# Last V group as the stationary side, last K loaded one transfer earlier, output projections as quarters: a decode-attention kernel whose end alone is not bound by DMA

## The chip, the cores and the metric

The kernel runs on one core of one Trainium2 chip. The metric is the device time of one execution in microseconds (us). Each ratio below is against the kernel before on the same chip in the same rounds; kernels of different batches are compared through it. Single executions of one kernel differ by up to 3 us (0.2%). The device time of an execution is 1.8 us longer than the span from its first to its last profiled instruction (1318.72 against 1316.9 us for the profiled one before); traces and table rows marked "span" give the shorter number.

## The reference

```python
# x [8,1,576]; k_cache, v_cache [8,32,4096,128]; wq [576,4096]; wo [4096,576]; all bf16
q = (x @ wq).reshape(8, 1, 32, 128).transpose(0, 2, 1, 3)
p = softmax(einsum("bhqd,bhkd->bhqk", q, k_cache) * 128 ** -0.5)
a = einsum("bhqk,bhkd->bhqd", p, v_cache)...reshape(8, 1, 4096) @ wo
b = gelu(layernorm(x) @ w1 + b1) @ w2 + b2
g = sigmoid((x * gate_w).sum(-1))
out = g * a + (1 - g) * b
```

K and V together are 537 MB and are read once. Everything else is small.

## The kernel before

One group is one batch element and four heads: 64 groups (`g` = 0 to 63), each with 4 MiB of K and 4 MiB of V, each in two alternating buffers. Partition 32h+p holds 128 keys of head h. The vector engine multiplies K by q, the matrix engine (PE) adds up the products in four chunks (`mult`), the vector engine reduces them (`reduce`), softmax follows. In a matrix product, one operand is loaded into PE as weights (the stationary side) and the other is streamed through (the moving side); a column tile is one of the four groups of 32 output partitions to which a small product can be sent (four of them start within 0.01 us of each other in the trace before, at 1305.91). The results stand in an accumulation memory (`psb` in the traces) until they are copied out (evicted). The values product has the probabilities as the stationary side (16 columns) and V as the moving side (512 columns); its result must be evicted and gathered by further matmuls.

```python
def pv(g, part, parts):                      # values product
    s = g % 2
    for land, t0, t1 in v_land[g]:
        ...
            p_pv[g] = matmul(o_ps[s][32*j:32*j+16, :], lhsT=P[:, s, 4 key slots, :],
                             rhs=VB[s][:, 4 key slots, :])        # 32 of them, on four column tiles
    v_done[g] = p_pv[g]                      # releases the V buffer

def evict(g): ...                            # scalar engine: o_ps -> O_sb
def gather(g): ...                           # 4 fp32 matmuls (8 passes): O_sb -> oz_ps, O transposed
def total(g): ...                            # ones matmul: sums of the probabilities over partitions
def norm(g): ...                             # reciprocal, multiply -> OT_sb

for g in range(NG):                          # NG = 64
    if g >= 1:
        if g + 1 < NG:
            load_k(g + 1)                    # waits for k_done(g-1)
            load_v(g)                        # waits for v_done(g-2)
        else:
            load_v_pieces(g)                 # last V in pieces of 64, 32, 16, 16 key slots
    def between(c):                          # behind chunk c of the scores on PE
        if c == 0 and g >= 2: gather(g - 2)
        if c == 1 and g >= 1: rowsum(g - 1); norm(g - 2); total(g - 1)
        if c == 2: ...                       # pieces of the projections
        if c == 3 and g >= 1: pv(g - 1, 0, 1); evict(g - 1)
    scores(g, between)
    if g + 1 < NG: q_of(g + 1)
    softmax(g)
gather(62); norm(62); rowsum(63); total(63); pv(63, 0, 1); evict(63); gather(63); norm(63)
a_proj(7)              # last four heads: 8 matmuls, 8-column weights, 288 moving columns
...                    # two output operations on 8 x 288, one store
```

(`gather(62)` and the like stand for the source's `gather(NG - 2)`; the matmul calls are shortened.)

## Time and profile before

| | before |
|---|---|
| time, median of the first three runs | 1317.06 us (1316.98 to 1318.01) |
| span of the profiled execution | 1316.9 us |
| DMA | 557.76 MB, mean 424 GB/s |
| last K landed / exponentials of group 63 end | 1284.1 / 1304.6 us |
| last piece of V landed | 1303.2 us |

From the page of the kernel before: busy shares, two rows of the 40 slices (busy tenths, and GB/s), and the chain of waits.

```profile
PE 897.5 (68%) x5204; PEld 428.9 (33%) x5204; DVE 871.6 (66%) x1058; ACT 204.5 (16%) x394; POOL 2.3 (0%) x11
...
DMA  9999999999999999999999999999999999999994
GB/s 398 428 429 430 431 430 429 429 430 433 432 429 431 433 428 430 420 427 430 430 430 430 432 430 432 433 431 430 431 430 431 430 430 429 431 432 431 432 433 190
...
DMA 64%; DVE 18%; PE 17%; ACT 1%; issue 0%; SPq 0%
```

DMA is full in 39 of 40 slices. Only the last slice is open. The transfer view of the last 77 us of the kernel before (from 1240 us, 1.93 us a digit) shows it more finely:

```profile
DMA  9999799998989999899998989989955510000000
GB/s 443 443 417 477 340 477 392 443 494 357 494 374 460 447 392 494 374 460 426 392 511 349 477 357 443 455 375 404 375 247 230 234 81 0 0 9 0 0 0 5
```

Seven of the 16 DMA engines have run ahead and are done by about 1297 us. The other nine finish near 1303 us. The last 13.5 us carry no K or V at all. The timeline of the kernel before, from the issue of the last V (start, duration, engine, line, operation, and in brackets the idle time before it and what ended it):

```profile
1281.32 2.29 SPq L183 DMA_DIRECT2D VB<-in_A_v_cache_dram  x4
...
1284.12 4.49 DVE L342 TENSOR_TENSOR p<-KB,q_bc 128x4096 bf16<-128x4096 bf16 x2 [2.70 <-DMA KB<-in_A_k_cache_dram]
...
1299.70 1.90 PE L402 MATMUL psb<-VB,P 128*16 128x512 bf16 x32
...
1302.28 2.33 ACT L384 ACTIVATE P<-s_sb,mD 32x128 bf16<-32x128 f32 x4
...
1304.64 0.69 DVE L390 TENSOR_REDUCE rs<-P 128x4 f32<-128x512 bf16 x1 [0.85 <-ACT P L384]
...
1305.91 3.59 PE L402 MATMUL psb<-VB,P 128*16 128x512 bf16 x32
...
1309.55 0.60 ACT L415 ACTIVATE O_sb<-psb 128x512 f32<-128x512 f32 x1 [4.94 <-PE psb L402]
...
1310.20 1.87 PE L420 MATMUL psb<-sel,O_sb 128*128 128x4 f32 x8 [0.70 <-ACT O_sb L415]
...
1312.56 2.08 PE L486 MATMUL psb<-RB,OT_sb 128*8 128x288 bf16 x8 [0.49 <-DVE OT_sb L427]
1313.71 0.51 DVE L551 SCALAR_TENSOR_TENSOR out_sb<-psb,stat,up 8x288 bf16<-8x288 f32 x1 [1.21 <-PE psb L486]
1314.67 0.50 DVE L551 SCALAR_TENSOR_TENSOR out_sb<-psb,stat,up 8x288 bf16<-8x288 f32 x1 [0.45 <-PE psb L486]
1315.21 0.31 SPq L183 DMA_DIRECT2D out_dram<-out_sb  x1
```

The reader should see one chain: the last K lands, scores and softmax take 20 us, and all of V has landed before its probabilities are ready. So the end of this kernel waits for the K side. The V side has slack: the last completion write of V comes at 1303.2, and the four matmuls that alone need the last piece start only at 1308.9.

### The profile page before, as it was taken

What the parts mean: (1) busy time and instruction counts of PE and PEld (TensorE: products, weight loads), DVE (VectorE), ACT (ScalarE), POOL (GpSimd) and SP (SyncE); (2) the same over time, 40 slices, a digit from 0 to 9 for tenths busy, and PEclk for the clock granted to TensorE, in tenths of its full rate; (3) what the DMA queues carried; (4) which work ended last, traced back from release to release, by engine and by line L of the source; (5) the groups of instructions that cost most, each with busy time, mean ns of one, the idle gap of its engine ahead of it and who ended that gap; (6) DMA issues with size and microseconds to landing.
All of it is one profiled execution on the core that took longest, in us unless ns stands there. A gap on an engine that the chain in (4) does not pass through costs nothing.

```text
span 1316.9 us, 12176 instructions
## 1 busy us (share of the span) xinstructions
PE 897.5 (68%) x5204; PEld 428.9 (33%) x5204; DVE 871.6 (66%) x1058; ACT 204.5 (16%) x394; POOL 2.3 (0%) x11
## 2 busy tenths in 40 slices
PE   3457776787748678647776676686666676586667
PEld 1123443343323334323333233232233233233323
DVE  3576676676747676746676776776676677667664
ACT  1201111111110110101111101101101101111111
POOL 0000000000000000000000000000000000000000
PEclk8777878868778798767877877878887887877786
DMA  9999999999999999999999999999999999999994
GB/s 398 428 429 430 431 430 429 429 430 433 432 429 431 433 428 430 420 427 430 430 430 430 432 430 432 433 431 430 431 430 431 430 430 429 431 432 431 432 433 190
DMA packets 24726, 557.76 MB, mean 424 GB/s; under 512 B 2368, under 2 KB 6496, under 8 KB 7008
## 3 DMA queue, kind: packets, MB, share of 16 engines
q1 hardware_dynamic: 24496, 556.95, 98.7%
q8 instruction: 41, 0.67, 0.2%
q14 instruction: 13, 0.11, 0.0%
q10 hardware_dynamic: 176, 0.03, 0.0%
HBM read 556.96 MB, written 0.01 MB: 423 GB/s over the span
## 4 chain that ended last, share of the span: by engine, by line
DMA 64%; DVE 18%; PE 17%; ACT 1%; issue 0%; SPq 0%
DMA KB<-in_A_k_cache_dram 64%; DVE p L342 14%; PE psb L352 13%; PE psb L420 3%; DVE s_sb L357 3%; PE psb L402 1%; ACT P L384 0%; DVE rz L426 0%; DVE OT_sb L427 0%; ACT O_sb L415 0%; PE psb L486 0%; SPq L183 0%; ACT L455 0%; DVE rs L390 0%; PE psb L409 0%
## 5 line engine op out<-in xcount | busy, mean ns | idle before, releaser
L352 PE MATMUL psb<-p,ident 128*128 128x512 bf16 x2048 | 651.1, 476 | 398.5 <-DVE p L342 398.5
L342 DVE TENSOR_TENSOR p<-KB,q_bc 128x4096 bf16<-128x4096 bf16 x256 | 579.6, 2285 | 177.8 <-DMA KB<-in_A_k_cache_dram 174.8
L352 PEld LDWEIGHTS psb<-p,ident 128*128 128x128 bf16 x2048 | 226.4, 121 | 713.0 <-DVE p L342 430.6
L357 DVE TENSOR_REDUCE s_sb<-psb 128x32 f32<-128x512 f32 x256 | 175.7, 687 | 106.1 <-PE psb L352 105.5
L415 ACT ACTIVATE O_sb<-psb 128x512 f32<-128x512 f32 x64 | 38.2, 597 | 1065.4 <-PE psb L402 1065.4
L384 ACT ACTIVATE P<-s_sb,mD 32x128 bf16<-32x128 f32 x256 | 147.0, 574 | 5.8 <-DVE mD L381 1.9
L402 PE MATMUL psb<-VB,P 128*16 128x512 bf16 x2048 | 123.5, 383 | 0.0
L420 PEld LDWEIGHTS psb<-sel,O_sb 128*128 128x128 f32 x512 | 106.1, 287 | 24.5 <-issue 16.7
L426 DVE RECIPROCAL rz<-psb 128x4 f32<-128x4 f32 x64 | 11.7, 183 | 137.1 <-PE psb L420 137.1
L420 PE MATMUL psb<-sel,O_sb 128*128 128x4 f32 x512 | 92.1, 303 | 1.4 <-ACT O_sb L415 1.4
L402 PEld LDWEIGHTS psb<-VB,P 128*16 128x16 bf16 x2048 | 45.9, 90 | 71.8 <-issue 28.4
L390 DVE TENSOR_REDUCE rs<-P 128x4 f32<-128x512 bf16 x64 | 43.5, 680 | 0.9 <-ACT P L384 0.9
L409 PEld LDWEIGHTS psb<-rs,ones 128*128 128x128 f32 x128 | 31.3, 245 | 18.0 <-issue 9.5
L409 PE MATMUL psb<-rs,ones 128*128 128x4 f32 x128 | 21.1, 235 | 2.0 <-DVE rs L390 2.0
L440 PEld LDWEIGHTS psb<-yT_sb,RB 128*128 128x128 bf16 (+1 forms) x216 | 19.4, 165 | 3.3
L336 ACT ACTIVATE q_bc<-psb 128x128 bf16<-128x128 f32 x64 | 17.4, 272 | 18.3 <-PE psb L334 18.3
L440 PE MATMUL psb<-yT_sb,RB 128*128 128x8 bf16 (+1 forms) x216 | 19.8, 227 | 0.0
L375 DVE TENSOR_REDUCE mA<-s_sb 128x1 f32<-128x128 f32 x64 | 18.3, 287 | 2.2
L334 PEld LDWEIGHTS psb<-Q,Sel 128*128 128x128 bf16 x64 | 6.1, 95 | 27.3 <-issue 26.7
L381 DVE STREAM_TRANSPOSE mD<-mC 128x32 f32<-128x32 f32 x64 | 13.5, 211 | 2.2
L377 DVE STREAM_TRANSPOSE mB<-mA 128x32 f32<-128x32 f32 x64 | 13.5, 211 | 2.2
L334 PE MATMUL psb<-Q,Sel 128*128 128x128 bf16 x64 | 14.7, 230 | 0.0
(56 smaller groups left out, 95.9 us busy)
## 6 DMA issues: line engine op xcount, KB each, us to landing
KB<-in_A_k_cache_dram SPq DMA_DIRECT2D x64, 4096.0 KB, 26.0
VB<-in_A_v_cache_dram SPq DMA_DIRECT2D x63, 4096.0 KB, 31.6
RB<-in_B_w_dram SPq DMA_DIRECT2D x1, 5184.0 KB, 43.5
RB<-in_B_w_dram SPq DMA_DIRECT2D x1, 4608.0 KB, 36.8
RB<-in_A_wo_dram SPq DMA_DIRECT2D x1, 4608.0 KB, 43.7
RB<-in_A_wq_dram SPq DMA_DIRECT2D x1, 4096.0 KB, 12.8
VB<-in_A_v_cache_dram SPq DMA_DIRECT2D x1, 2048.0 KB, 17.4
VB<-in_A_v_cache_dram SPq DMA_DIRECT2D x1, 1024.0 KB, 19.5
```

Source lines behind the costliest of these rows:

```text
L334: t = op("tensor", lambda e: e.matmul(qb_ps[:, 0:DH], lhsT=Sel[:, b, :], rhs=Q4[:, hg * DH:(hg + 1) * DH], start=True, stop=True), [a_Q[hg ...
L342: v_mult[g, c] = op("vector", lambda e: e.tensor_tensor(out=p1[:, par, :, :], in0=KB[s][:, c * CT:(c + 1) * CT, :], in1=qb, op=ALU.mult), ...
L352: p_sum[g, c] = op("tensor", lambda e, r=r, n=n: e.matmul(tr_ps[par][:, :], lhsT=ident[:, :], rhs=r, start=(n == 0), stop=(n == NCH - 1)), w)
L357: v_red[g, c] = op("vector", lambda e: e.tensor_reduce(out=s_sb[:, s, c * CT:(c + 1) * CT], in_=tr_ps[par][:, :].rearrange("p (t c) -> p t ...
L375: t = op("vector", lambda e: e.tensor_reduce(out=mA[:, 0:1], in_=s_sb[:, s, :], axis=AX.X, op=ALU.max), [v_red[g, NCK - 1], c_mA])
L384: a_exp[g] = op("scalar", lambda e, h=h, q=q: e.activation(out=P[q, s, :, h], in_=s_sb[q, s, :], func=ACT.Exp, bias=mD[q, s, 0:1], scale=1.0),
L390: v_rs[g] = op("vector", lambda e: e.tensor_reduce(out=rs[:, s, :], in_=P[:, s, :, :].rearrange("p t h -> p h t"), axis=AX.X, op=ALU.add), ...
L402: p_pv[g] = op("tensor", lambda e, o=o, tq=tq: e.matmul(o, lhsT=P[:, s, tq * TQ:(tq + 1) * TQ, :].rearrange("p t h -> p (t h)"), rhs=VB[s] ...
L409: p_z[g] = op("tensor", lambda e: e.matmul(oz_ps[:, HB:2 * HB], lhsT=ones[:, :], rhs=rs[:, g % 2, :], start=True, stop=True), [v_rs[g], v_ ...
L415: a_ev[g] = op("scalar", lambda e: e.activation(out=O_sb[:].rearrange("p t d -> p (t d)"), in_=o_ps[s][:, :], func=ACT.Copy), [p_pv[g], p_ ...
L420: p_oz[g] = op("tensor", lambda e, tt=tt: e.matmul(oz_ps[:, 0:HB], lhsT=O_sb[:, tt, :], rhs=sel16[:, tt, :], start=(tt == 0), stop=(tt == ...
L440: st["p_up"] = op("tensor", lambda e, w=w, o=o, kt=kt: e.matmul(o, lhsT=w, rhs=yT_sb[:, kt, :], start=(kt == 0), stop=(kt >= NKF)), [*ld_w ...
```

## The change

The intent has three parts.

1. Order: K(63) is loaded before V(61), so that the last scores can start earlier. `pv`, `evict` and `gather` of groups 61 and 62 move with it.
2. Turned product: for group 63, each slot of 128x128 V is the stationary side and four columns of probabilities are the moving side. O comes out transposed, so the last eviction and gather vanish. V comes in seven pieces.
3. Quarters: the down and output projections use 144 columns on each of four column tiles. The output operation works on 104 partitions, and four stores go out on two queues.

```diff
-    V_LAST = (64, 32, 16, 16)
+    V_LAST = (32, 32, 16, 16, 16, 8, 8)
...
+    def quarters(lhsT, w, first, stop, waits):
+        for i in range(4):
+            last = op("tensor", lambda e, i=i: e.matmul(
+                y_ps[32 * i:32 * i + B, 0:QN], lhsT=lhsT, rhs=w[:, i * QN:(i + 1) * QN], start=first, stop=stop),
+                waits if i == 0 else ())
+        return last
...
+    def pv_turned(g, pieces):
+        s = g % 2
+        for n in pieces:
+            land, t0, t1 = v_land[g][n]
+            for t in range(t0, t1):
+                p_oz[g] = op("tensor", lambda e, t=t: e.matmul(
+                    o_ps[s][:, 0:HB], lhsT=VB[s][:, t, :], rhs=P[:, s, t, :], start=(t == 0), stop=(t == NTT - 1)),
+                    [land, a_exp[g], a_ev.get(g - 2)] if t == t0 else ())
...
-        if g >= 1:
-            if g + 1 < NG:
-                load_k(g + 1)
-                load_v(g)
-            else:
-                load_v_pieces(g)
+        if 1 <= g <= NG - 3:
+            load_k(g + 1)
+        if 1 <= g <= NG - 2 and g != NG - 3:
+            load_v(g)
...
             if c == 2:
...
+                if g == NG - 1:
+                    pv(NG - 3, 0, 1)
+                    evict(NG - 3)
+                    load_v_pieces(g)
             if c == 3:
-                if g >= 1:
+                if 1 <= g < NG - 2:
                     pv(g - 1, 0, 1)
                     evict(g - 1)
+                if g == NG - 1:
+                    gather(NG - 3)
...
         scores(g, between)
+        if g == NG - 3:
+            load_k(g + 2)
+            load_v(g)
...
+    last = NG - 1
+    norm(last - 2)
+    pv(last - 1, 0, 1)
+    evict(last - 1)
+    total(last - 1)
+    rowsum(last)
+    pv_turned(last, (0,))
+    gather(last - 1)
+    norm(last - 1)
+    pv_turned(last, (1,))
+    total(last)
+    recip(last)
+    pv_turned(last, range(2, len(V_LAST)))
+    norm_turned(last)
```

Cut: the renaming of the PSUM banks (the parts of the accumulation memory), smaller guards in `between`, the gate and bias spread to four partition groups, the output operation and the four stores.

More of the change, by code (lines that the diff above doesn't have):

```diff
@@ L30 @@
 TQ = 4
+QN = D // 4
+QP = 96 + B
 NTQ = NTT // TQ
@@ L144, in bass_gated_mix__mha_block_cached__mixer_channel_mlp__decode_kernel @@
     b1_sb = sb("b1_sb", [128, NJ], BF16)
-    b2_8 = sb("b2_8", [B, D], BF16)
+    b2_4 = sb("b2_4", [128, QN], BF16)
     hT_sb = sb("hT_sb", [128, NJ, B], BF16)
@@ L151, in bass_gated_mix__mha_block_cached__mixer_channel_mlp__decode_kernel @@
     OT_sb = sb("OT_sb", [128, H, B], BF16)
-    bmg_sb = view(up, 0, [B, D])
-    out_sb = sb("out_sb", [B, D], BF16)
+    bmg_sb = view(up, 0, [128, QN])
+    out_sb = sb("out_sb", [128, QN], BF16)
+    g4 = sb("g4", [128, 2], F32)
     ident = sb("ident", [128, 128], BF16)
@@ L174, in bass_gated_mix__mha_block_cached__mixer_channel_mlp__decode_kernel @@
     oz_ps = bank[5]
-    xy_ps = bank[6:8]
+    up_ps = bank[6]
+    y_ps = bank[7]
     YT_COL = 64
@@ L190, in bcast @@
         return bass.AP(tensor=t.tensor, offset=t.offset, ap=[[0, B], [1, D]])
+    c_b2 = op("gpsimd", lambda e: e.memset(b2_4[:], 0.0))
+    c_g4 = op("gpsimd", lambda e: e.memset(g4[:], 0.0))
     ld_x = load("sync", x_sb, x_flat, "ld_x")
     ld_gw = load("scalar", gw8, bcast(gate_w), "ld_gw")
-    ld_b2 = load("scalar", b2_8[:, :], bcast(B_b2), "ld_b2")
+    ld_b2 = [load("scalar", b2_4[32 * i:32 * i + B, :],
+                  bass.AP(tensor=B_b2.tensor, offset=B_b2.offset + i * QN, ap=[[0, B], [1, QN]]), f"ld_b2{i}", [c_b2])
+             for i in range(4)]
     ld_b1 = load("scalar", b1_sb[:, :], B_b1.rearrange("(p j) -> p j", j=NJ), "ld_b1")
@@ L254, in bass_gated_mix__mha_block_cached__mixer_channel_mlp__decode_kernel @@
     c_ps = [memset("vector", bank[i][:, :], 0.0) for i in range(4)]
+    c_yps = memset("vector", y_ps[:, :], 0.0)
     c_sel16 = op("vector", lambda e: e.tensor_reduce(
@@ L288, in transposed @@
         for kt in range(NKF + 2):
-            o = xy_ps[0][:, col + kt * B:col + (kt + 1) * B]
+            o = up_ps[:, col + kt * B:col + (kt + 1) * B]
             i = src[:, kt * 128:(kt + 1) * 128] if kt < NKF else srcz[:, kt - NKF, :, :].rearrange("b r s -> b (r s)")
@@ L296, in untransposed @@
         return op("vector", lambda e: e.tensor_copy(
-            out=dst.rearrange("p k b -> p (k b)"), in_=xy_ps[0][:, col:col + (NKF + 2) * B]), waits)
+            out=dst.rearrange("p k b -> p (k b)"), in_=up_ps[:, col:col + (NKF + 2) * B]), waits)
     v_xz = spread(xz, x_sb, [ld_x])
@@ L306, in bass_gated_mix__mha_block_cached__mixer_channel_mlp__decode_kernel @@
                                                    scalar1=-1.0, scalar2=1.0, op0=ALU.mult, op1=ALU.add), [a_g])
+    for i in range(4):
+        v_g4 = op("vector", lambda e, i=i: e.tensor_copy(out=g4[32 * i:32 * i + B, :], in_=stat[:, G_COL:G_COL + 2]),
+                  [v_omg, c_g4])
     v_yz = spread(yz, y_sb, [v_y])
@@ L327, in bass_gated_mix__mha_block_cached__mixer_channel_mlp__decode_kernel @@
              load("sync", w1_t, halves(B_w1), "ld_w1b")]
-    a_qb, v_mult, v_red, p_sum, v_nm, a_exp, p_pv, a_ev, p_oz, v_norm, v_rs, p_z = ({} for _ in range(12))
+    a_qb, v_mult, v_red, p_sum, v_nm, a_exp, p_pv, a_ev, p_oz, v_norm, v_rs, p_z, v_rz = ({} for _ in range(13))
     def q_of(g):
@@ L435, in up_proj @@
             for kt in range(NKF + 2):
-                o, n, at = xy_ps[0][:, jt * B:(jt + 1) * B], 128, kt * F + jt
+                o, n, at = up_ps[:, jt * B:(jt + 1) * B], 128, kt * F + jt
                 if kt >= NKF:
-                    o, n, at = xy_ps[0][64 * (kt - NKF):64 * (kt - NKF) + 64, jt * B:(jt + 1) * B], 64, NKF * F + jt
+                    o, n, at = up_ps[64 * (kt - NKF):64 * (kt - NKF) + 64, jt * B:(jt + 1) * B], 64, NKF * F + jt
                 w = bass.AP(tensor=RB, offset=at, ap=[[pstride(RB), 128], [NJ, n]])
@@ L447, in act_h @@
         t = op("vector", lambda e: e.tensor_tensor(
-            out=hb.rearrange("p (f b) -> p f b", b=B), in0=xy_ps[0][:, 0:NJ * B].rearrange("p (f b) -> p f b", b=B),
+            out=hb.rearrange("p (f b) -> p f b", b=B), in0=up_ps[:, 0:NJ * B].rearrange("p (f b) -> p f b", b=B),
             in1=b1b, op=ALU.add), [st["p_up"], ld_b1])
@@ L460, in load_w2 @@
         st["ld_w2"] = load("sync", w2_sb, B_w2.rearrange("(p j) n -> p j n", j=NJ), "ld_w2", [st["p_up"]])
+    def quarters(lhsT, w, first, stop, waits):
+        for i in range(4):
+            last = op("tensor", lambda e, i=i: e.matmul(
+                y_ps[32 * i:32 * i + B, 0:QN], lhsT=lhsT, rhs=w[:, i * QN:(i + 1) * QN], start=first, stop=stop),
+                waits if i == 0 else ())
+        return last
     def down_proj(j0, j1):
         for jt in range(j0, j1):
-            for half in range(2):
-                st["p_down"] = op("tensor", lambda e, jt=jt, half=half: e.matmul(
-                    xy_ps[half][0:B, 0:288], lhsT=hT_sb[:, jt, :], rhs=w2_sb[:, jt, half * 288:(half + 1) * 288],
-                    start=(jt == 0), stop=(jt == NJ - 1)), [st["ld_w2"], st["v_h"], st["v_hb"]] if jt == 0 else ())
+            st["p_down"] = quarters(hT_sb[:, jt, :], w2_sb[:, jt, :], jt == 0, jt == NJ - 1,
+                                    [st["ld_w2"], st["v_h"], c_yps] if jt == 0 else ())
     def b_out():
-        last = None
-        for half in range(2):
-            q = slice(half * 288, (half + 1) * 288)
-            last = op("vector", lambda e, half=half, q=q: e.tensor_tensor(
-                out=bmg_sb[:, q], in0=xy_ps[half][0:B, 0:288], in1=b2_8[:, q], op=ALU.add), [st["p_down"], ld_b2])
-        st["v_bx"] = last
+        st["v_bx"] = op("vector", lambda e: e.tensor_tensor(
+            out=bmg_sb[0:QP, :], in0=y_ps[0:QP, 0:QN], in1=b2_4[0:QP, :], op=ALU.add), [st["p_down"], *ld_b2])
         st["v_bmg"] = op("vector", lambda e: e.tensor_scalar(
-            out=bmg_sb[:, :], in0=bmg_sb[:, :], scalar1=stat[:, OMG_COL:OMG_COL + 1], scalar2=None, op0=ALU.mult),
-            [last, v_omg])
+            out=bmg_sb[0:QP, :], in0=bmg_sb[0:QP, :], scalar1=g4[0:QP, 1:2], scalar2=None, op0=ALU.mult),
+            [st["v_bx"], v_g4])
     def load_wo():
@@ L483, in a_proj, with recip, norm_turned @@
     def a_proj(hg):
-        for half in range(2):
-            for h in range(hg * HB, (hg + 1) * HB):
-                st["p_a"] = st["p_a", half] = op("tensor", lambda e, h=h, half=half: e.matmul(
-                    xy_ps[half][0:B, 0:288], lhsT=OT_sb[:, h, :], rhs=wo_sb[:, h, half * 288:(half + 1) * 288],
-                    start=(h == 0), stop=(h == H - 1)), [v_norm[hg * B + B - 1], st["ld_wo"], st["v_bx"]])
+        for h in range(hg * HB, (hg + 1) * HB):
+            st["p_a"] = quarters(OT_sb[:, h, :], wo_sb[:, h, :], h == 0, h == H - 1,
+                                 [v_norm[hg * B + B - 1], st["ld_wo"], st["v_bx"]] if h == hg * HB else ())
+    def pv_turned(g, pieces):
[6 more added lines that the diff above has]
+                    [land, a_exp[g], a_ev.get(g - 2)] if t == t0 else ())
+    def recip(g):
+        v_rz[g] = op("vector", lambda e: e.reciprocal(out=rz[:, :], in_=oz_ps[:, HB:2 * HB]), [p_z[g]])
+    def norm_turned(g):
+        hg, b = divmod(g, B)
+        v_norm[g] = op("vector", lambda e: e.tensor_tensor(
+            out=OT_sb[:, hg * HB:(hg + 1) * HB, b], in0=o_ps[g % 2][:, 0:HB], in1=rz[:, :], op=ALU.mult),
+            [p_oz[g], v_rz[g]])
     UP0, UPN = 3, 12
@@ L496, in bass_gated_mix__mha_block_cached__mixer_channel_mlp__decode_kernel @@
     for g in range(NG):
-        if g >= 1:
-            if g + 1 < NG:
-                load_k(g + 1)
-                load_v(g)
-            else:
-                load_v_pieces(g)
+        if 1 <= g <= NG - 3:
+            load_k(g + 1)
+        if 1 <= g <= NG - 2 and g != NG - 3:
+            load_v(g)
         def between(c, g=g):
-            if c == 0 and g >= 2:
+            if c == 0 and 2 <= g < NG - 1:
                 gather(g - 2)
@@ L508, in between @@
                 rowsum(g - 1)
-                if g >= 2:
-                    norm(g - 2)
-                total(g - 1)
+                if g < NG - 1:
+                    if g >= 2:
+                        norm(g - 2)
+                    total(g - 1)
             if c == 2:
@@ L536, in bass_gated_mix__mha_block_cached__mixer_channel_mlp__decode_kernel @@
         softmax(g)
-    gather(NG - 2)
-    norm(NG - 2)
-    rowsum(NG - 1)
-    total(NG - 1)
-    pv(NG - 1, 0, 1)
-    evict(NG - 1)
-    gather(NG - 1)
-    norm(NG - 1)
+    last = NG - 1
[12 more added lines that the diff above has]
+    norm_turned(last)
     while done_a[0] < NHG:
@@ L547, in bass_gated_mix__mha_block_cached__mixer_channel_mlp__decode_kernel @@
         done_a[0] += 1
-    last = []
-    for half in range(2):
-        q = slice(half * 288, (half + 1) * 288)
-        last.append(op("vector", lambda e, half=half, q=q: e.scalar_tensor_tensor(
-            out=out_sb[:, q], in0=xy_ps[half][0:B, 0:288], scalar=stat[:, G_COL:G_COL + 1], in1=bmg_sb[:, q],
-            op0=ALU.mult, op1=ALU.add), [st["p_a", half], st["v_bmg"], a_g]))
-    ld_out = load("sync", out_flat, out_sb[:, :], "ld_out", last)
-    S.ops["sync"].append([lambda e: None, [ld_out], None, None])
+    t = op("vector", lambda e: e.scalar_tensor_tensor(
+        out=out_sb[0:QP, :], in0=y_ps[0:QP, 0:QN], scalar=g4[0:QP, 0:1], in1=bmg_sb[0:QP, :],
+        op0=ALU.mult, op1=ALU.add), [st["p_a"], st["v_bmg"]])
+    ld_out = [load(("sync", "scalar")[i % 2], out_flat[:, i * QN:(i + 1) * QN], out_sb[32 * i:32 * i + B, :],
+                   f"ld_out{i}", [t]) for i in range(4)]
+    S.ops["sync"].append([lambda e: None, ld_out, None, None])
     S.resolve()
```

## The prediction

> **What bounds the kernel now.** DMA. The page shows 557 MB at 424 GB/s with the DMA row at 9 in 39 of 40 slices; matrix engine 68% busy, vector engine 66%. The chain of waits is 64% K transfers. Only the end is not DMA-bound. The transfer view of the last stretch shows the 16 engines full until 1295.7 us, about nine of 16 busy until 1303, then nothing; the span ends at 1316.9. So the change can only reach about 13.5 us, 1%.
>
> **Why that tail exists.** In the chain and the timeline, the last K lands at 1284.1, scores and softmax of the last group run to 1304.6 (after the last V has landed), then: row sum and ones matmul 1.3, values matmuls 3.6 (half clock), eviction 0.6, gather 1.9, normalisation 0.4, eight 128x8 by 288 projection matmuls 2.1, last output operation 0.5, store 1.75.
>
> **What changes.**
> 1. The last K is fetched ahead of V(61), so it lands near 1274 instead of 1284. It cannot be used then: the vector engine is in group 62 until 1281.4. So the last scores start only about 2.7 us earlier (1281.4). They also lose a gather (1.7) and norm between their chunks: about 2 us more. Exponentials end near 1300-1302.5 instead of 1304.6.
> 2. A new wait: V(63) needs the buffer of V(61), and its values matmuls now stand behind the third chunk of the last scores, near 1292-1295 (before, the issue was at 1281.3). V(62) is in by 1293.5, so DMA idles 1-4 us, and the last piece lands near 1305-1307 instead of 1303.5.
> 3. The last values product: 128 matmuls with a 128x128 V weight and 4 columns, in place of 32 of 512. In the trace the transposes of x (contiguous 128-column bf16 weights) stand 27 ns apart, the strided up-projection 60 ns. The Trainium skill, "TensorE: Matmul & The Clock Gate", section on weight-path modes, says full 128-column non-fp32 weights load fast; the 27 ns agree. Estimate: 128 x 27-55 ns (full or half clock) = 3.5-7 us, most of it under the landing of the pieces. Eviction and gather of the last group (2.5 us) leave the chain.
> 4. Projection of the last four heads as quarters on four column tiles: 2.1 to about 0.7-1.0; output operation 0.5 to 0.35; store of four pieces on two queues 1.75 to about 2.3 (issues are 0.6 us apart).
>
> **Sum.** Full clock: last landing 1305.2, last eight tiles 0.4, norm 0.3, projection 0.7, output 0.4, store 2.3: 1309.3. Half clock with exponentials at 1301: values, gather(62) and ones matmuls 9.5, then 4: 1314.6. The clock view shows half clock at the end of before, after a 2 us idle gap. I take the middle: **1311.5 us** (0.4% faster), range 1307 to 1316. Chances: faster by over 2% 0.005, within 2% 0.985, slower 0.01.
>
> **What would show it.** (1) First multiply of the last group at about 1281.4 ended by the previous softmax, not by a K landing. (2) The issue of the last V pieces waiting for the values matmuls, near 1293, and a hole in the DMA row before the last V. (3) 128-column V weights 27-55 ns apart. (4) From the last values matmul to the end under 4.5 us.
>
> **What would make it wrong.** Weight loads at 60-110 ns (then 1316 or more); a later V issue because the half clock stretches the sums; a different drift of the DMA engines, which moves the end by a microsecond or more.

## The result, and the profile after

| | before | changed |
|---|---|---|
| median of the runs beside each other | 1317.53 us (1316.98 to 1318.78) | 1314.45 us (1313.47 to 1314.88) |
| ratio | | 0.9974 (0.9957 to 0.9992) |
| ratio, repeated in other rounds | | 0.9967 (0.9954 to 0.9979) |
| span of the profiled execution | 1316.9 us | 1313.1 us |

The time lies inside the predicted range, 3 us above the predicted point. Of these 3 us, 1.8 are no matter of mechanism: the prediction added up times of the profile, so its sum is a span, while the measured time is device time.

The transfer view of the changed kernel from 1240 us:

```profile
DMA  9899998965999999999999989650069999800000
GB/s 494 357 485 409 396 494 357 477 272 255 409 392 443 409 443 494 392 443 409 443 426 460 443 374 477 281 255 34 0 179 421 434 398 417 324 15 0 5 0 0
```

Where the kernel before thinned out at the end, the changed one has a hole of about 5 us around 1294, and then runs with all 16 engines until about 1307. Its timeline:

```profile
1265.08 4.49 DVE L354 TENSOR_TENSOR p<-KB,q_bc 128x4096 bf16<-128x4096 bf16 x2 [2.62 <-DMA KB<-in_A_k_cache_dram]
...
1282.74 4.45 DVE L354 TENSOR_TENSOR p<-KB,q_bc 128x4096 bf16<-128x4096 bf16 x2
...
1293.46 1.90 PE L414 MATMUL psb<-VB,P 128*16 128x512 bf16 x32
...
1295.41 3.46 SPq L187 DMA_DIRECT2D VB<-in_A_v_cache_dram  x7
...
1299.21 2.34 ACT L396 ACTIVATE P<-s_sb,mD 32x128 bf16<-32x128 f32 x4 [3.20 <-DVE mD L393]
...
1301.70 0.94 PE L508 MATMUL psb<-P,VB 128*128 128x4 bf16 x32 [1.56 <-ACT P L396]
...
1307.74 0.94 PEld L508 LDWEIGHTS psb<-P,VB 128*128 128x128 bf16 x24 [2.09 <-DMA VB<-in_A_v_cache_dram]
1307.75 1.02 PE L508 MATMUL psb<-P,VB 128*128 128x4 bf16 x24 [2.01 <-DMA VB<-in_A_v_cache_dram]
1309.02 0.29 PEld L508 LDWEIGHTS psb<-P,VB 128*128 128x128 bf16 x8 [0.34 <-DMA VB<-in_A_v_cache_dram]
1309.03 0.37 PE L508 MATMUL psb<-P,VB 128*128 128x4 bf16 x8 [0.25 <-DMA VB<-in_A_v_cache_dram]
1309.44 0.18 DVE L517 TENSOR_TENSOR OT_sb<-psb,rz 128x4 bf16<-128x4 f32 x1 [4.44 <-PE psb L508]
...
1309.67 0.65 PE L477 MATMUL psb<-RB,OT_sb 128*8 128x144 bf16 x16 [0.27 <-DVE OT_sb L517]
1310.37 0.37 DVE L593 SCALAR_TENSOR_TENSOR out_sb<-psb,g,up 104x144 bf16<-104x144 f32 x1 [0.76 <-PE psb L477]
```

Three things are to be seen. First, the last multiplies (1282.74) follow the softmax of group 62 with no wait for a transfer: K(63) was there. Second, the values matmuls of group 61 (L414 at 1293.46) stand on PE behind the third chunk of the last scores, and the seven V pieces are issued the moment they end (1295.41, against 1281.32 before). Third, the exponentials are done at 1301.6, 3 us earlier than before, but PE then waits for V. The last piece lands at 1308.5, 5.3 us later than before. What the order won at the probabilities it lost at V, and the end is now on the V side. The sync engine's waits of the changed kernel, from 1200 us, name the releaser (waiter, what it waited for, total us, times, longest):

```profile
SPq L187 <- PE psb L414: 32.7, 1, 32.7
```

### The profile page after: what moved, and what is told of

It is laid out like the page before. It is cut to its first block, busy times and chain, and to the rows that moved or that the text cites. A ratio compares the mean times of both kernels' runs of the same rounds, so it can differ in the third digit from the quotient of the medians.

```text
span 1313.1 us, 12641 instructions
## 1 busy us (share of the span) xinstructions
PE 877.7 (67%) x5428; PEld 419.8 (32%) x5428; DVE 871.2 (66%) x1061; ACT 204.1 (16%) x393; POOL 2.5 (0%) x13
## 4 chain that ended last, share of the span: by engine, by line
DMA 65%; DVE 18%; PE 16%; ACT 0%; issue 0%; SPq 0%
DMA KB<-in_A_k_cache_dram 64%; DVE p L354 14%; PE psb L364 13%; PE psb L432 3%; DVE s_sb L369 3%; DMA VB<-in_A_v_cache_dram 1%; PE psb L414 0%; SPq L187 0%; DVE rz L438 0%; DVE OT_sb L439 0%; ACT P L396 0%; ACT L467 0%; ACT O_sb L427 0%; PE psb L477 0%; DVE mA L387 0%
## 5 line engine op out<-in xcount | busy, mean ns | idle before, releaser
L414 PE MATMUL psb<-VB,P 128*16 128x512 bf16 x2016 | 119.9, 379 | 0.0
L432 PEld LDWEIGHTS psb<-sel,O_sb 128*128 128x128 f32 x504 | 101.9, 280 | 21.3 <-issue 16.3
L432 PE MATMUL psb<-sel,O_sb 128*128 128x4 f32 x504 | 88.2, 298 | 0.0
L414 PEld LDWEIGHTS psb<-VB,P 128*16 128x16 bf16 x2016 | 44.7, 89 | 69.9 <-issue 26.3
```

Of the source, the lines that this page charges most:

```text
L414: p_pv[g] = op("tensor", lambda e, o=o, tq=tq: e.matmul(o, lhsT=P[:, s, tq * TQ:(tq + 1) * TQ, :].rearrange("p t h -> p (t h)"), rhs=VB[s] ...
L432: p_oz[g] = op("tensor", lambda e, tt=tt: e.matmul(oz_ps[:, 0:HB], lhsT=O_sb[:, tt, :], rhs=sel16[:, tt, :], start=(tt == 0), stop=(tt == ...
```

## The experiments

The theory formed from the two traces (A): the end is set by the landing of the last V. The landing is late because its buffer is released by a product that the PE program order put late. A rival (B): the landing is bound to come then, by the total of the bytes and the drift of the DMA engines, and the gain came from the other parts. Ten runs were made (nine other kernels, and the changed one again), each timed in five rounds; all gave correct results. The diffs of experiments 3 to 6 are shortened, some with group numbers in place of `NG` and `last`. Readings of their profiled executions, in us ("landed" is the last completion write of V in the trace; the profile's own landing, on which PE waits, is 0.4 to 0.5 us later):

| kernel | exponentials end | first V piece issued | last V landed | span | ratio to before (95%) |
|---|---|---|---|---|---|
| before | 1304.6 | 1281.3 | 1303.2 | 1316.9 | 1 |
| changed | 1301.6 | 1295.4 | 1308.5 | 1313.1 | 0.9974 (0.9957-0.9992) |
| changed, again | 1299.3 | 1293.2 | 1306.4 | 1311.0 | 0.9967 (0.9954-0.9979) |
| order only | 1299.4 | 1293.2 | 1305.2 | 1312.7 | 0.9976 (0.9964-0.9989) |
| order and turned | 1299.6 | 1293.5 | 1306.6 | 1312.1 | 0.9972 (0.9959-0.9984) |
| old order, turned and quarters | 1304.3 | 1280.9 | 1304.1 | 1312.1 | 0.9979 (0.9965-0.9992) |
| quarters only | 1305.5 | 1282.3 | 1303.8 | 1315.4 | 1.0001 (0.9988-1.0013) |
| changed, V(63) in K buffer | 1299.7 | 1277.4 | 1304.3 | 1309.1 | 0.9946 (0.9934-0.9959) |
| order only, V(63) in K buffer | 1298.8 | 1276.9 | 1303.3 | 1310.8 | 0.9967 (0.9954-0.9981) |
| changed, values of 61 after first chunk | 1300.4 | 1289.3 | 1303.9 | 1309.4 | 0.9949 (0.9935-0.9963) |
| order only, 96 idle matmuls | 1298.7 | 1292.6 | 1305.7 | 1314.2 | 0.9982 (0.9969-0.9995) |
| V(63) in K buffer, eviction moved | 1299.7 | 1277.5 | 1303.9 | 1308.4 | 0.9944 (0.9931-0.9956) |

### 1. The last V into the buffer of the last but one K

```diff
-            dst, part = VB[s][:, t0:t0 + nt, :], src[:, t0:t0 + nt, :]
-            t = load("sync", dst, part, f"sVl{n}", [v_done.get(g - 2)])
+            dst, part = KB[1 - s][:, t0:t0 + nt, :], src[:, t0:t0 + nt, :]
+            t = load("sync", dst, part, f"sVl{n}", [k_done[g - 1]])
...
-                    o_ps[s][:, 0:HB], lhsT=VB[s][:, t, :], rhs=P[:, s, t, :], ...
+                    o_ps[s][:, 0:HB], lhsT=KB[1 - s][:, t, :], rhs=P[:, s, t, :], ...
```

> The changed kernel, with one wait taken away: the last V goes into the buffer of the last but one K, which is free at about 1279 us, instead of the buffer of V(61), which is free only at 1295.4. Nothing else moves. Theory A (the late issue of the last V opens the DMA hole and sets the end): the last V pieces are issued near 1280, the hole at 1291-1297 vanishes, the last piece lands at 1303.5-1304.5 instead of 1309.0, and the end is then set by the exponentials (end at 1301.5) plus about 5 us of matrix work plus 3.7 us of epilogue: a span near 1310.3, about 0.995 of before. Theory B (the landing of the last piece is set by the total of the bytes and the drift of the DMA engines, and the issue had slack): the last piece still lands at 1308-1309 and the span stays at 1313, 0.997.

Measured: 0.9946, 1310.42 us median. The pieces were issued at 1277.4, and the last one landed at 1304.3. The transfer view of this kernel from 1240 us, and the timeline around the last V product:

```profile
DMA  9899998978999899998999979998996530000000
GB/s 460 374 485 426 413 460 374 460 340 323 426 392 511 357 494 392 426 494 357 494 392 443 494 323 438 438 404 370 406 414 248 230 139 10 0 5 0 0 0 0
```

```profile
1277.40 3.26 SPq L187 DMA_DIRECT2D KB<-in_A_v_cache_dram  x7
...
1303.46 1.85 PE L508 MATMUL psb<-P,KB 128*128 128x4 bf16 x64
```

The hole is gone, and the last 64 matmuls no longer wait for a transfer. The fair profile to set beside this one is the repeat of the changed kernel, whose exponentials also end early (1299.3): the landing is 2.1 us earlier and the span 1.9 us shorter. A holds and B falls: the edit changes no other instruction, and the time went from 0.9974 and 0.9967 to 0.9946. The intervals of this run and of both runs of the changed kernel do overlap a little (by 0.0002 and 0.0005), but the executions do not: all five here took 1310.25 to 1310.85 us, all nine of the changed kernel 1312.76 to 1314.88 (the kernel before had medians of 1317.5 to 1318.0 in all these batches). Experiment 2 takes the same wait away in another way and agrees.

### 2. The values product of group 61 behind the first chunk instead of the third

```diff
+            if c == 0 and g == NG - 1:
+                pv(NG - 3, 0, 1)
+                evict(NG - 3)
+                load_v_pieces(g)
...
             if c == 2:
...
-                if g == NG - 1:
-                    pv(NG - 3, 0, 1)
-                    evict(NG - 3)
-                    load_v_pieces(g)
```

> The changed kernel with one move: the values matmuls of group 61, and with them the release of the V buffer, stand behind the first chunk of the last scores instead of the third. No other buffer is used. They then run near 1285.6-1287.5 (full clock), the last V pieces are issued near 1287.5 instead of 1293.2-1295.4, when the first engines have just drained, and the hole in the transfers is nearly gone. The sums of the second chunk wait 2 us for them, but the reduction they feed has slack, so the exponentials end within 0.5 us of 1299.4. Theory A (the place of this product in the matrix engine's order is the whole cost of the hole): the last piece lands near 1304.3, span 1309.3, ratio 0.9945 as with the K buffer. Theory B (the older V buffer itself is the trouble, its release is always late): 0.997 as the changed kernel.

```profile
1286.66 2.62 PE L414 MATMUL psb<-VB,P 128*16 128x512 bf16 x32
...
1289.33 3.93 SPq L187 DMA_DIRECT2D VB<-in_A_v_cache_dram  x7
...
1303.84 1.85 PE L508 MATMUL psb<-P,VB 128*128 128x4 bf16 x64
```

Measured: 0.9949 (1310.87 to 1311.43 us). The pieces were issued at 1289.3, 1.8 us later than expected: the granted matrix clock was 0.50 from 1284.8 to 1288.2, and the values product took 2.62 us where it took 1.90 in the changed kernel. The exponentials ended at 1300.4, the last piece landed at 1303.9, and again PE did not wait for it. So the old buffer is good enough: the place of one product in the matrix engine's order was the cost.

### 3. The parts alone: order, quarters, and turned with quarters

`order_only` is the kernel before with the load order and the moved `pv`, `evict`, `gather` of the diff, and nothing else:

```diff
 (kernel before, with the loop of the change)
+    norm(61); pv(62, 0, 1); evict(62); total(62); rowsum(63); gather(62); norm(62)
+    total(63); pv(63, 0, 1); evict(63); gather(63); norm(63)
```

> The kernel before with the new load order alone (old product, old four last pieces, old projections). Theory A: the last V is issued only near 1295 and lands near 1308; then values, eviction, gather, norm (3.3 us) and the old epilogue (4.4 us) follow: a span of 1316 to 1317.5, 0.999 to 1.001 of before. Theory B (order carries the gain): 1314.5 or less, 0.998 or less.

This expectation was wrong: measured 0.9976, as good as the whole change within the intervals. In its profiled execution K(62) was used 1.2 us earlier (1263.9 against 1265.1) and the sums of the first two chunks took 5.31 us. In the first profile of the changed kernel they took 6.31, with the granted clock at 0.50 until 1290.5 and here until 1287.9. So the last V was issued at 1293.2 rather than the 1295 that I had copied from that trace. It landed 11.9 us after that, not 13. I had taken a single execution for the rule.

`old_order_turned_quarters` is the other half of the change:

```diff
 (changed kernel, with the loop and the loads of before)
+    gather(62); norm(62); rowsum(63); pv_turned(63, (0, 1)); total(63); recip(63)
+    pv_turned(63, range(2, 7)); norm_turned(63)
```

> The changed kernel with the loads and the order of the work of before; the turned product, the smaller last pieces and the quarters are kept. Theory A (the load order gained nothing net: what it won at the exponentials it lost at the last V): the last K lands at about 1284, the exponentials end at 1304.6 with all of V there, 128 turned matmuls of 25-29 ns take 3.5 us, then norm and epilogue 3.9: a span near 1313, within 1 us of the changed kernel, 0.997 of before. Theory B (the load order carries most of the gain): 1315.5 or more, 0.999.

Measured 0.9979; the profiled span was 1312.1. So each half alone gives about what both give together, 0.9979 and 0.9976 against 0.9974 and 0.9967. The timing alone does not rule out that the two gains add up (0.9979 times 0.9976 is 0.9955, below the interval of the first run of the changed kernel and just inside that of the repeat). The traces show why they do not: the limit moves. With the old order the end hangs on the exponentials (1304.3): the turned product starts behind them and never waits for V. With the new order it hangs on the last V. The timelines of `old_order_turned_quarters` and of `order_only`:

```profile
1304.41 1.84 PE L508 MATMUL psb<-P,VB 128*128 128x4 bf16 x64 [1.40 <-ACT P L396]
...
1306.54 1.85 PE L508 MATMUL psb<-P,VB 128*128 128x4 bf16 x64
```

```profile
1293.23 1.86 SPq L183 DMA_DIRECT2D VB<-in_A_v_cache_dram  x4
...
1305.66 0.39 PE L402 MATMUL psb<-VB,P 128*16 128x512 bf16 x4 [0.49 <-DMA VB<-in_A_v_cache_dram]
```

The third run takes the quarters alone:

> The kernel before with the quarters alone (projections, output operation, stores). From the end of the last normalisation to the end of the span: 4.4 us before, 3.5 us in the changed kernel, so a gain of about 0.9 us: a span near 1316.0, 0.9993 of before. The last four heads' matmuls shrink from 2.1 to about 0.7 us, and the four stores on two queues give back 0.5 us. If the body of the kernel profits from quarters too, it is more than that; I expect not, as DMA bounds it.

The edit is the quarters' hunks of the diff, put into the kernel before with its four pieces. Measured 1.0001 (0.9988 to 1.0013): no effect that the timing can resolve. The trace does show the shorter end: from the end of the last normalisation to the end of the span 3.2 us (1312.2 to 1315.4) against 4.4 before (1312.5 to 1316.9). The expected 0.9993 lies inside the interval, so this run settles nothing more. `order_turned` against the repeated changed kernel, with landings 0.2 us apart, points the same way: spans of 1312.1 and 1311.0.

### 4. Is the late landing of the changed kernel an accident?

In the first profile of the changed kernel the last V landed 13.1 us after its issue, in that of the order alone 11.9 us. Two reruns asked whether this belongs to the program. The first is the changed kernel itself; the second leaves the quarters out:

> The changed kernel unchanged, once more, beside the others on one chip. Of its first profile two things may be accidents of that execution: the last but one K landed 1.4 us later than in the profile of the order alone, and a packet of instruction fetch (16 KB, 1.05 us) at 1305.6 held back one DMA engine and with it the last three V pieces by about 1.5 us. Theory A: the fetch belongs to the program (256 more matrix instructions at its end), so it falls into the last V transfer again and the last piece lands 13 us or more after the first V piece is issued; span 1312.5-1313.5, ratio 0.997. Theory B (accident): the last piece lands within 12 us of the issue as in the run of the order alone, and the ratio is 0.996 or less.

> The changed kernel without the quarters: the new load order and the turned product (with the seven pieces), old projections, output operation and store. If the parts that follow the last landing add up, it lies between the order alone and the changed kernel: turned saves about 2 us after the landing (last part 0.4, eviction 0.6, gather 1.1, reciprocal 0.2, less 0.4 for eight tiles), quarters 1.0 to 1.2. Theory A: the seven pieces with the instruction fetch in their midst land later than the four pieces of the order alone and give most of it back: ratio 0.9975 to 0.9985, no better than the order alone (0.9976). Theory B (they add up): 0.996.

```diff
 (order_turned: order_only, plus)
+    V_LAST = (32, 32, 16, 16, 16, 8, 8), pv_turned, recip, norm_turned and the tail of the change
```

Measured: 13.2 and 13.1 us from issue to landing. In these two profiles and in the first of the changed kernel, one packet of the queue "instruction" falls into the last V transfer. In the order alone none falls inside it: one starts at 1305.11, when only the last completion write (1305.16) is outstanding. From the transfer views of the changed kernel (1295 to 1309 us) and of the order alone (1293 to 1305 us), queue lines (queue and kind: packets, MB, share of 16 engines):

```profile
q1 hardware_dynamic: 1008, 4.19, 76.8%
q8 instruction: 1, 0.02, 0.5%
```

```profile
q1 hardware_dynamic: 572, 4.19, 88.9%
```

The packet has 16,384 bytes and took 1.05 us (at 1305.58 in the changed kernel, 1303.38 in its repeat). The completion writes of the repeat show one engine late. A list of them, worked out from the trace, in us:

```
last piece: most of its 16 writes at 1304.6 to 1304.9; the last three writes of all at 1305.1, 1305.7, 1306.4
```

The last three writes are 0.65 us apart, which is one engine bringing its shares of the last three pieces behind the others. The expected span of the repeat (1312.5 to 1313.5) was missed: it was 1311.0, as V was issued 2.2 us earlier than in the first profile. The timed part of the expectation was 0.997 for the repeat (measured 0.9967), and 0.9975 to 0.9985 for `order_turned` (measured 0.9972, between the two theories' numbers, the interval covers both).

### 5. Making the instruction fetch fall into the last V of the order alone

```diff
     total(62)
+    for _ in range(96):
+        matmul(qb_ps[:, 0:4], lhsT=ident, rhs=ident[:, 0:4])      # of no use, PE is idle here
     rowsum(63)
```

> The order alone with 96 matmuls of no use (identity weights, 4 columns, an unused bank) in the idle time of the matrix engine before the last gather of group 62. They change no data and no transfer. Theory A (the number of matrix instructions near the end brings an instruction fetch of 16 KB into the last V transfer, which holds one DMA engine for 1.05 us): a fetch packet starts between 1294.5 and 1304, one engine's last V parts land 0.8 to 1.5 us after the others, the last landing comes 12.8-13.4 us after the first V piece is issued instead of 11.9, and the end moves by about 1.0 us: span 1313.7, ratio 0.9983. Theory B (the late engine in the three profiles with the turned product has another cause): landing 11.9 us after the issue, ratio 0.9976.

Measured: 0.9982, a fetch packet of 1.00 us at 1301.09, and the last V 13.1 us after its first issue. All completion writes of the last piece came by 1304.4 except one, at 1305.7. The queue lines of this kernel's transfer view (1293 to 1305.8 us):

```profile
q1 hardware_dynamic: 577, 4.19, 83.3%
q8 instruction: 1, 0.02, 0.5%
```

So 192 more matrix instructions (96 matmuls and their weight loads), which touch no data that matters, put a fetch into the last transfer, and the time from issue to landing grew by 1.2 us. As V was issued 0.6 us earlier here, the landing itself is only 0.5 us later than in the order alone. The rest of the longer span (1.5 us) is not the fetch: after the last values matmul the clock was low in this execution, and the last gather took 1.87 us instead of 1.06. The intervals of the two timed ratios overlap, so the timed loss is not shown on its own; the late engine is.

The fetch is no rival to the hole as the cause of the late end. A fetch falls into the last V transfer of experiments 1 and 2 too (1302.5 and 1302.7), and they gain all the same. In experiment 1 it did not move the landing: the last engine is 0.7 to 0.8 us behind the others on all seven pieces, before the fetch and after it.

The trace of the kernel before also says something of where the drift of the engines comes from. For each K and V load, take how far each of the 16 completion events lies behind the first, and add them up: 3.2 us at 34 us into the kernel, 71 us at 1286 us. Up to 1265 us this sum stays within 0.4 us from one load to the next in 76 cases and rises by more in 46, of which 38 rise by 1.4 us or more; there are 39 instruction fetches of 16 KB and 12 of 8 KB in that time. A fetch starts while the two loads of a step land in 45 of the 46 rises, and in 24 of the 76 others. (Once, near 577 us, the sum falls, by 4.5 us.) So the last 7 us with nine of 16 engines look like the sum of the fetches. No run took the fetches away, so this is read from the trace and not tested.

### 6. The K buffer under the old product, and a better version

> The order alone, with the last V in the buffer of the last but one K: old product, old pieces, old projections. The exponentials end near 1299.4 and the last piece lands near 1303.5-1304 instead of 1305.1, so the end moves by about 1.2 us: a span near 1311.5, ratio 0.9967. If the wait for the V buffer cost the old product as much as it cost the changed kernel (3.7 us), the ratio would be 0.995.

The edit is that of experiment 1, on `order_only`. Measured 0.9967; V landed at 1303.3 and the span was 1310.8. The gain over the order alone (0.0009) is smaller than under the turned product (0.0021 to 0.0028), as expected, though the intervals overlap. In the trace, the 32 products with 512 columns took 3.22 us and did not wait for V.

> The candidate: the changed kernel with the last V in the K buffer, and the eviction of group 62 on the vector engine, which is idle there, so that its gather (1.6 us) leaves the stretch between the exponentials and the last tiles. Exponentials end at 1299.8; 128 tiles and the ones matmul take 4.0 us: 1303.8, so the end is set by the last landing (1304.3) plus 0.3 plus 3.7 us: span 1308.3, ratio 0.9939 to 0.9945, 0.5 us under the run without the moved eviction. If the landing binds fully already, no difference (0.9946).

```diff
-    evict(last - 1)                 # scalar engine, behind the four exponentials of group 63
+    evict_dve(last - 1)             # vector engine, idle here; gather and norm of 62 move before pv_turned
```

Measured 0.9944, against 0.9946 without the moved eviction: no difference in the timing (medians 1310.38 and 1310.42), 0.7 us in the profiled spans. The PE waits of at most 0.3 us for V pieces are back in its timeline, so the landing (1303.9) binds again and there is little left to win. This version is correct and beats both kernels: before by 0.56%, and the changed one in the same rounds by 2.7 us (1310.38 against 1313.07 us, medians).

## Why the prediction was right or wrong

- **The bound (right).** DMA bounds the body. The change reached only the last 13.5 us, and the result (0.3%) lies under that limit (1%).
- **Step 1, the earlier exponentials (right).** Predicted start of the last multiplies 1281.4, released by the softmax before and not by K: measured 1282.7 and 1281.2. Predicted end of the exponentials 1300 to 1302.5: measured 1301.6 and 1299.3 (the repeat is 0.7 us below the range).
- **Step 2, the new wait (right in kind, too small in size).** Issue predicted at 1292 to 1295, measured 1295.4 and 1293.2. Landing predicted at 1305 to 1307 and put into the full-clock sum as 1305.2; measured 1308.5 and 1306.4. This is the term of the sum that was mis-sized. "DMA idles 1-4 us" was also too small for the first profile: between 1286 and 1298 the 16 engines idled 5.1 us each on the mean, 3.8 in the repeat (worked out from the packets). About 1.2 us of the late landing is the instruction fetch, which the prediction did not have at all.
- **Step 3, the turned product (right at full clock, wrong at half clock).** Predicted 27 to 55 ns for each matmul. Measured from start to start: 25.2 ns in a full-clock stretch (the first 32 matmuls of the changed kernel, 1301.7 to 1302.6, granted clock 1.00) and 26.7 ns in a half-clock one (the last 64 of experiment 1, 1303.5 to 1305.3, granted 0.50). The clock hardly matters here. In experiment 1, where PE did not wait for V, it took 5.6 us from the exponentials to the last values matmul (1299.7 to 1305.3, half clock from 1301.0), where the half-clock branch had 9.5. The fast load agrees with the Trainium skill ("TensorE: Matmul & The Clock Gate", section "Weight-path perf modes — Fast Weight Load (FWL) and DoubleRow"), and the same page's section "Wait — 56ns, not 53.3ns?" states a floor of about 25 ns from start to start however few the columns; the 25.2 ns agree. A floor does not say what half the clock does; only the measured 26.7 ns take the half-clock branch (1314.6) away.
- **Step 4, the epilogue (right).** Predicted under 4.5 us from the last values matmul to the end; measured 3.7 (1309.4 to 1313.1).
- **The sum.** 1311.5 was about the mean of a branch that was too low (1309.3, the landing) and one that was wrong (1314.6, half-clock weights). As spans, which is what the sum is made of, the changed kernel took 1313.1 and 1311.0 us. The full-clock branch with the measured landings (1308.5 and 1306.4 in place of 1305.2) gives 1312.6 and 1310.5, so the landing is nearly the whole of its error. That the middle came so near was partly luck: the two errors had opposite signs.

## What to carry to other kernels

When loads are reordered, a buffer's release moves with the instruction that releases it, so look up where that instruction stands in its engine's program order before the reorder is trusted; here one product two chunks too late cost 0.0018 to 0.0025 of the time, about as much as the reorder won (0.0024). At the end of a DMA-bound kernel, two chains (the last operand's landing and the work that must precede it) take turns as the limit, so parts that each give a quarter of a per cent need not add up. A buffer of another stream that has just come free can take the last transfer; here no run shows a cost of that.

## What the Trainium skill lacked or had wrong

- "Runtime: NRT & Kernel Launch", section "Instruction fetch mechanics", says that instructions are refilled in 16 KiB blocks and that the cost is mostly hidden. The trace agrees with the size (packets of 16,384 bytes), but the packet takes one of the 16 DMA engines for about 1.07 us (median of 41 in the kernel before, 0.96 to 1.11). Inside a transfer that all engines share and that the end waits for, the landing moved by 1.2 us (13.1 against 11.9 us after issue).
- "TensorE: Matmul & The Clock Gate", section on weight-path modes, gives the fast load for packed and strided columns alike. In the trace of the kernel before, most of the up-projection's strided 128-column weights (a step of 36 elements) stood 60 ns apart at a granted clock of 1.00; the packed ones of the turned product 25 ns. No run tried the stride alone, so other differences between the two are not excluded. The page does not say that a turned product of this kind is nearly free of the clock: 25.2 ns at full, 26.7 ns at half.
- "DMA: Bandwidth & Descriptors", section "Why a DMA increments its semaphore by 16 and not by 1", has that the engines finish independently, and the trace agrees. It does not say how far they drift apart under one long queue: completions of one K or V load lay 0.6 us apart at 34 us into the kernel before and about 8 us apart at its end, so the last transfer ran for about 7 us with nine of 16 engines. Nor does it name what goes along with the drift here, the instruction fetches (experiment 5).
